# Nyström attention, expert FFN and GLU in one kernel: ScalarE first for steps that two engines can do, one-hot rows by one comparison a batch, batch 1's queries and keys in freed slots, new ranks for the planner

## The chip, the cores and the metric

The kernel runs on one core of a Trainium2 chip. The metric is the device time of one execution in microseconds (us), given as the median of three runs. The core has a matrix engine (TensorE, PE in the profile; PEld is its weight load), VectorE (DVE), ScalarE (ACT), GpSimd (POOL) and a queue engine, SyncE (SP), which here only issues DMAs and loads registers. PE, DVE and ACT read and write PSUM, the small memory in which matmuls accumulate; a 2 KB piece of it is a bank.

## The reference, cut to what matters

Four batches of 576 tokens with 8 heads of 64; 32 landmarks; an inverse by six iterations; then every token goes to the expert with the largest router logit (8 experts, at most 576 tokens each), through that expert's FFN, and what comes out through a gated layer (GLU).

```python
    A = sm(q, k_lm)
    Bm = sm(q_lm, k_lm)
    C = sm(q_lm, k)
    Z = ...
    for _ in range(6):
        Z = 2 * Z - Z @ Bm @ Z
    return (A @ Z @ C @ v).astype(np.float32)
...
    expert_idx = np.argmax(logits, axis=1)
...
    h = np.maximum(np.einsum('ecd,edf->ecf', disp, w1), 0.0)
    y = np.einsum('ecf,efd->ecd', h, w2)
...
            out[i] = gate_w[i] * y[expert_idx[i], pos[i]]
...
    gate = 1.0 / (1.0 + np.exp(-(x @ w_gate)))
    val = x @ w_val
    return (gate * val @ w_out).astype(np.float32)
```

## The kernel before, in words

**Stages.** First the attention, batch by batch, then blocks of up to 576 tokens of one expert through FFN and GLU. With these inputs three blocks have work: the *lead* block, whose tokens come from batch 0 alone and whose FFN starts while the later batches are still in attention; block 1; and one pass of a loop over the rest. The matmuls of blocks work on values split into a high and a low part, three products for one.

**Names of the attention.** For every batch `load_qk` brings q and k from memory in tiles named `qk` (or `slot`), `load_v` brings v (`early<-in_v`). PE transposes them (`pt<-ident,qk`), and the result is copied to `qT` and `kT`. Landmark sums are made on GpSimd (`s`). Scores are the matmuls `pa`, `pb` and `pc`, with row maxima through `pm`/`pnb`, exponentials `ea`, `eb` and `ec`, transposes `pct` copied to `ct`, and products with v in `pv`, copied to `cp`. The inverse's iterations alternate `py` (copied to `y`), `pu` and an update of `z`. `px` are the rows of the attention's output, scaled by the gate into `xt` and stored to memory (`x_rows`, and `x_lead` for batch 0).

**Routing.** For each batch the place of every token in the expert lists is worked out on VectorE, and a table of token numbers is made by a matmul of two one-hot matrices, `ptb<-hi,lo`. For each of six token columns there is one `hi` (which of 160 table columns) and one `lo` (which of 128 partitions). Once batch 0's table stands, SyncE reads the lead expert's number into a register, its weights are loaded (`w_raw`), and GpSimd gathers the lead block's rows by five indirect DMAs (`slot<-x_lead`).

**Blocks.** FFN: `mm<-xa,ws` and the like go through three PSUM banks. GLU: for every hidden tile a gate product and a value product go to a bank each; ScalarE takes the sigmoid of the gate product (`sg<-mm`), VectorE multiplies it with the value product (`sg<-mm,sg`), both split it, and `acc<-ws,...` is its product with the output weights. `ws_68` to `ws_71` and others hold split weights, made from `early` or `w_raw`. While the first GLU runs, its weights arrive as `raw_g`, `raw_v` and `raw_o` in an interleaved layout, and ScalarE separates and rounds them (`ACTIVATE raw_g<-raw_g`); `narrow` is the code for that. At the end of a block, `o_tile<-acc` copies the sums and `out<-o_tile` scatters them.

**What sets the order.** No order is written by hand. Every piece of work is a Python generator, and the class `Streams` runs them all against a clock of its own. Each `yield` names the engine and the things that the next step needs. `start` works out when the step could begin, `go` takes the one with the least planned start plus `SLACK` (0.003) times its rank from the table `URGENCY`, and `settle` adds the planned costs. Ranks so differ by some hundredths of a microsecond. A step for engine `any` may run on VectorE or ScalarE; before, it goes to the one that could begin it first. `fill_up` puts matmuls that compute nothing (`idle<-ones,ident`) into planned gaps of PE when the planned activity of the array is low. The order on each engine is thus fixed when the program is built, and an instruction waits for whatever stands ahead of it in its engine's row. All those instructions have line 88 in the profile. DMAs keep their own lines: 820 q and k, 833 v, 855 zeros, 490 interleaved weights, 557 expert weights, 1486 attention rows, 422 gathers, 723 scatters.

**Zeros.** The output has rows that no block writes. `zero_rows` stores zeros over the whole output in six DMAs of 768 KB, from a tile in the attention's own pool; before, it is spawned when batch 1's v is loaded and waits for the first load of the last batch's q.

**Buffers for q and k.** Batch 0 loads into eight `slot` tiles that are later used by the blocks; the other batches load into `qk` tiles from a pool of few, and each load needs one of these free (`raw`).

Of the kernel before, what the change touches and what calls it, by code (L numbers as in the profile page):

```python
# [10 lines left out]
F32 = mybir.dt.float32  # L11
F32R = mybir.dt.float32r
# [15 lines left out]
    sums=20,  # L28
    landmarks=30,
    transposes=0,  # L30
    inverse=4,
    scores=8,
    context=3,
    back=3,
    weights=15,
    rows=6,
    lead_rows=1,
    lead_loads=4,
    lead_split=15,
    lead=20,  # L40
    narrow=25,
# [51 lines left out]
class Streams:  # L93
# [5 lines left out]

    LAG = 0.2  # L100
    SAME = 0.13
# [99 lines left out]
    def settle(self, at, engine):  # L201
        first = True
        for what, name, value, columns in self.log:
            if what == "run":
# [7 lines left out]
                if name == "pe":  # L212
# [6 lines left out]
                    self.recent.append((at, columns))  # L219
                at += value  # L220
# [51 lines left out]
def tile_attention_moe_glu(  # L272
# [55 lines left out]
    wt = [wsp.tile([128, 2, 4, 128], F32R, name=f"ws{i}") for i in range(4)]  # L328
    actx = ExitStack()
# [156 lines left out]
    def narrow(dst, src, name):  # L486
# [4 lines left out]
        on.took("sp", 1.9)  # L491
# [50 lines left out]
    def expert_loads(b, number, at, split_urgency, first=0, until=KF + 2 * KD, needs=()):  # L542
# [4 lines left out]
        for i in range(first, until):  # L547
# [11 lines left out]
            run.took("sp", 0.95)  # L559
# [202 lines left out]
    with actx:  # L762
# [4 lines left out]
        zeros = ap.tile([128, 128], F32, name="zeros")  # L767
        nc.gpsimd.memset(zeros, 0.0)
# [41 lines left out]
        def load_qk(b):  # L810
            for w, src in enumerate((q, k)):
                for i in range(H // 2):
                    yield "sp", *(["raw"] if b else [])
                    if b == 0:
# [9 lines left out]
                    run.took("sp", 0.85)  # L824
# [5 lines left out]
        def load_v(b):  # L830
# [3 lines left out]
            run.took("sp", 3.4)  # L834
# [7 lines left out]
            if b == 1:  # L842
                run.spawn(zero_rows(), 200)
# [4 lines left out]

        def zero_rows():

            rows = out.rearrange("(p r) d -> p (r d)", p=128)
            for c in range(6):
                n = N // 128 * D // 6
                yield "sp", f"raw{B - 1}00"
                nc.sync.dma_start(
                    rows[:, c * n : (c + 1) * n].rearrange("p (x d) -> p x d", d=128),
                    zeros.unsqueeze(1).broadcast_to([128, n // 128, 128]),
                )
                run.took("sp", 2.2)

        def transposes(b):

            halves = []
            for w in range(2):

                s1 = None
                for g in range(2):
                    for jj in range(3):
# [14 lines left out]
                        if jj == 2 and b:  # L883
                            run.release("raw", "raw")
                        run.later(
# [346 lines left out]
        def back(b):  # L1232
# [140 lines left out]
            dve.tensor_copy(cf, ci[:, 1:3])  # L1373
            for j in range(J):
# [195 lines left out]
    def free_slots(**kinds):  # L1570
        run.slots.update({kind: [0.0] * n for kind, n in kinds.items()})
# [108 lines left out]
```

## Time and profile before

| what | us |
|---|---|
| median of three runs | 683.87 |
| lowest and highest run | 681.34, 688.35 |
| the profiled execution | 686.8 |
| its span, first to last instruction | 682.8 |
| PE busy in the span | 647.4 (95%) |
| DVE, ACT, POOL busy | 400.8, 286.3, 99.3 |

The profiled execution is one more execution, of 686.8 us, of which 4.0 us lie outside the span. A busy time adds up the stretches in which an engine had an instruction in hand. The granted clock is the TensorE clock as a share of full speed, 2.4 GHz; at half of it, 1.2 GHz, a matmul takes longer.

### The profile page before, as it was taken

What the parts mean: (1) busy time and instruction counts of PE and PEld (TensorE: products, weight loads), DVE (VectorE), ACT (ScalarE), POOL (GpSimd) and SP (SyncE); (2) the same over time, 40 slices, a digit from 0 to 9 for tenths busy, and PEclk for the clock granted to TensorE, in tenths of its full rate; (3) what the DMA queues carried; (4) which work ended last, traced back from release to release, by engine and by line L of the source; (5) the groups of instructions that cost most, each with busy time, mean ns of one, the idle gap of its engine ahead of it and who ended that gap; (6) DMA issues with size and microseconds to landing.
All of it is one profiled execution on the core that took longest, in us unless ns stands there. A gap on an engine that the chain in (4) does not pass through costs nothing.

```text
span 682.8 us, 14185 instructions
## 1 busy us (share of the span) xinstructions
PE 647.4 (95%) x5628; PEld 573.9 (84%) x5628; DVE 400.8 (59%) x1045; ACT 286.3 (42%) x644; POOL 99.3 (15%) x165
## 2 busy tenths in 40 slices
PE   7898879999997999999999899999999999999995
PEld 4466447688897999999999799999989999999994
DVE  7678859988777878786534443334435244434432
ACT  3424245544346666664433433333334234323331
POOL 3473466110011000000002400000020030000002
PEclk9999989999999999999999999999999999999999
DMA  8572999714376575544001300000034120000001
GB/s 212 119 176 78 263 234 272 229 33 134 116 227 190 169 219 177 155 143 136 1 1 38 103 1 0 1 1 1 1 116 141 30 70 1 0 1 1 1 1 70
DMA packets 64897, 65.94 MB, mean 97 GB/s; under 512 B 3513, under 2 KB 59841, under 8 KB 64833
## 3 DMA queue, kind: packets, MB, share of 16 engines
q1 hardware_dynamic: 62160, 56.78, 29.4%
q0 software_dynamic: 2672, 8.27, 3.9%
q8 instruction: 45, 0.74, 0.5%
q14 instruction: 20, 0.16, 0.1%
HBM read 50.87 MB, written 14.16 MB: 95 GB/s over the span
## 4 chain that ended last, share of the span: by engine, by line
PE 65%; issue 18%; DVE 7%; DMA 5%; ACT 2%; POOL 1%; SPq 1%; POOLq 0%; DVEq 0%; ACTq 0%
PE mm L88 44%; PE acc L88 11%; DMA qk<-in_q 3%; PE pt L88 2%; DMA out<-o_tile,idx_now 1%; PE pc L88 1%; SPq L820 1%; PE pa L88 1%; DVE xt L88 1%; PE pv L88 1%; DMA qk<-in_k 1%; PE pct L88 1%; PE px L88 1%; DVE ea L88 1%; PE idle L88 1%
## 5 line engine op out<-in xcount | busy, mean ns | idle before, releaser
L88 PEld LDWEIGHTS mm<-xb,ws 128*128 128x128 f32 x1344 | 189.9, 189 | 13.1 <-ACT ws L88 2.9
L88 PE MATMUL mm<-xb,ws 128*128 128x288 f32 x1344 | 197.3, 297 | 3.2 <-ACT ws L88 2.2
L88 PE MATMUL mm<-xa,ws 128*128 128x288 f32 x960 | 142.6, 300 | 5.1 <-ACT sg L88 4.7
L88 PEld LDWEIGHTS mm<-xa,ws 128*128 128x128 f32 x960 | 133.7, 190 | 11.1 <-ACT sg L88 5.0
L88 PE MATMUL acc<-ws,slot 128*128 128x512 f32 x476 | 130.5, 393 | 0.0
L88 PEld LDWEIGHTS acc<-ws,slot 128*128 128x128 f32 x476 | 82.3, 188 | 9.2
L88 DVE TENSOR_TENSOR sg<-mm,sg 128x288 f32<-128x288 f32 x72 | 32.8, 455 | 91.3 <-PE mm L88 90.7
L88 PE MATMUL mm<-slot,ws 128*128 128x288 f32 x576 | 79.5, 296 | 0.0
L88 PEld LDWEIGHTS mm<-slot,ws 128*128 128x128 f32 x576 | 76.9, 188 | 1.1 <-issue 0.5
L88 ACT CAST slot<-sg 128x288 fp32r<-128x288 f32 x68 | 29.4, 432 | 80.1 <-DVE sg L88 80.1
L88 DVE TENSOR_TENSOR ws<-wo_res,ws 128x512 fp32r<-128x512 f32 x30 | 20.8, 692 | 48.6 <-ACT ws L88 48.6
L88 ACT CAST ws<-wo_res 128x512 fp32r<-128x512 f32 x30 | 18.6, 621 | 70.7 <-PE acc L88 69.3
L88 DVE TENSOR_TENSOR slot<-sg,slot 128x288 fp32r<-128x288 f32 (+2 forms) x102 | 33.5, 354 | 17.2 <-ACT slot L88 17.2
L723 POOL DMA_INDIRECT out<-o_tile,idx_now x10 | 10.2, 1018 | 223.1 <-DVE o_tile L88 215.5
L422 POOL DMA_INDIRECT slot<-x_rows,idx_next x10 | 10.5, 1054 | 214.3 <-ACT sg L88 163.4
L88 DVE TENSOR_TENSOR ws<-w_raw,ws 128x512 fp32r<-128x512 f32 x50 | 34.7, 695 | 11.2 <-ACT ws L88 10.9
L88 ACT ACTIVATE sg<-mm 128x288 f32<-128x288 f32 x72 | 29.4, 409 | 28.1 <-PE mm L88 28.0
L88 ACT CAST ws<-w_raw 128x512 fp32r<-128x512 f32 x50 | 30.8, 618 | 17.7 <-PE mm L88 17.2
L88 ACT ACTIVATE slot<-mm 128x288 fp32r<-128x288 f32 x48 | 19.6, 409 | 21.6 <-PE mm L88 21.5
L88 DVE SCALAR_TENSOR_TENSOR slot<-mm,slot 128x288 fp32r<-128x288 f32 x48 | 21.6, 450 | 6.1 <-ACT slot L88 5.8
L88 DVE TENSOR_TENSOR xb<-mm,xb 128x288 fp32r<-128x288 f32 (+2 forms) x21 | 10.5, 500 | 23.0 <-ACT xb L88 22.8
L88 PE MATMUL pt<-ident,qk 96*128 96x96 f32 x144 | 19.9, 265 | 3.8 <-DMA qk<-in_q 2.9
(262 smaller groups left out, 829.4 us busy)
## 6 DMA issues: line engine op xcount, KB each, us to landing
w_raw<-in_moe_w SPq DMA_DIRECT2D x50, 256.0 KB, 3.2
raw_g<-in_moe_w_gate SPq DMA_DIRECT2D x12, 512.0 KB, 3.9
raw_v<-in_moe_w_val SPq DMA_DIRECT2D x12, 512.0 KB, 5.6
raw_o<-in_moe_w_out SPq DMA_DIRECT2D x12, 512.0 KB, 3.8
early<-in_v SPq DMA_DIRECT2D x4, 1152.0 KB, 12.1
x_rows<-xt SPq DMA_DIRECT2D x12, 384.0 KB, 6.1
out<-zeros SPq DMA_DIRECT2D x6, 768.0 KB, 7.0
qk<-in_q SPq DMA_DIRECT2D x12, 288.0 KB, 4.4
```

Source lines behind the costliest of these rows:

```text
L88: return getattr(self.engine, op)(*args, **kwargs)
L422: nc.gpsimd.indirect_dma_start(rows[c][0:n], None, src[:, :], bass.IndirectOffsetOnAxis(ap=idx[0:n, c : c + 1], axis=0), bounds_check=n_sr ...
L723: scatter = nc.gpsimd.indirect_dma_start(out[:, :], bass.IndirectOffsetOnAxis(ap=idx[0:n, c : c + 1], axis=0), o[0:n], None, bounds_check= ...
L820: nc.sync.dma_start(t.rearrange("p h j d -> p h (j d)"), src[b, 2 * i : 2 * i + 2].rearrange("h (p j) d -> p h (j d)", j=J),)
```

## The change

Six edits, in the order of the diff.

1. `URGENCY` has new ranks (all but `load`, `transposes` and `context`).
2. The planner: an `any` step goes to ScalarE unless VectorE could begin it over 0.6 us earlier (`SPARED`); time planned on GpSimd puts off planned work of VectorE by 0.3 of it (`SHARED`); PE behind PE has no planned gap; and some planned costs of SP are higher.
3. The tile of zeros lies in the base pool.
4. Batch 1's q and k go to the eight slots, each as soon as batch 0's transposes of that tile are done (`turned0..`), instead of to the pool.
5. `zero_rows` is spawned ahead of the second part of the order, and its DMAs wait until the last of the interleaved output weights is done (`narrow_o11`).
6. `hi` is made for all six columns by one comparison on a 96 x 6 x 160 tile instead of by six of 96 x 160.

```diff
 URGENCY = dict(
     load=4,
-    sums=20,
-    landmarks=30,
+    sums=40,
+    landmarks=5,
...
-    narrow=25,
+    narrow=3,
...
+    SPARED = 0.6
     LAG = 0.2
+    SHARED = 0.3
...
         def begin(engine):
-            return max(ready + (self.SAME if engine == last else self.LAG if last else 0), self.free[engine])
+            return max(ready + (0 if engine == last == "pe" else self.SAME if engine == last else self.LAG if last else 0), self.free[engine])
 
         if engine == "any":
-            engine = min("dve", "act", key=begin)
+            engine = "dve" if begin("dve") + self.SPARED < begin("act") else "act"
...
+                if name == "pool":
+
+                    self.free["dve"] = max(self.free["dve"], at) + self.SHARED * value
...
+    zeros = base.tile([128, 128], F32, name="zeros")
+    nc.gpsimd.memset(zeros, 0.0)
...
-                    yield "sp", *(["raw"] if b else [])
-                    if b == 0:
+
+                    yield "sp", *(["raw"] if b > 1 else []), *([f"turned0{w}{i // 2}"] if b == 1 else [])
+                    if b < 2:
...
-            if b == 1:
-                run.spawn(zero_rows(), 200)
...
+            yield ("dve",)
+            hi = wk.tile([P, J, NCOL], F32R, tag="hi", name=f"hi{b}", bufs=1)
+            dve.tensor_tensor(
+                hi,
+                iota_c[0:P].unsqueeze(1).broadcast_to([P, J, NCOL]),
+                cf[:, 1].unsqueeze(2).broadcast_to([P, J, NCOL]),
+                ALU.is_equal,
+            )
...
-                hi = wk.tile([P, NCOL], F32R, tag="hi", name=f"hi{b}{j}", bufs=2)
...
-                dve.tensor_scalar(hi, iota_c[0:P], cf[:, 1, j : j + 1], None, ALU.is_equal)
...
+    def zero_rows():
...
+            yield "sp", f"narrow_o{KG - 1}"
...
+    run.spawn(zero_rows(), 200)
     run.spawn(first_units(), 0)
```

What stands on the engines changes with it. In the whole program ScalarE has 703 instructions instead of 638 and VectorE 987 instead of 1072; the fills (`idle`) are 29 with 11,031 columns instead of 21 with 5,942.

ScalarE at the first sigmoid of the lead block, before. `raw_g` are interleaved gate weights, `ws` split expert weights, the table load is what the sigmoid needs:

```order
L88 CAST xa<-mm 128x288 x2
L88 ACTIVATE raw_g_3593<-raw_g_3593 128x512
L88 CAST ws_3497<-early 128x512
L88 ACTIVATE raw_g_3593<-raw_g_3593 128x512
L88 ACTIVATE raw_g_3601<-raw_g_3601 128x512
L88 CAST ws_70<-early 128x512
L88 ACTIVATE raw_g_3601<-raw_g_3601 128x512
L88 ACTIVATE raw_g_3603<-raw_g_3603 128x512
L88 CAST ws_71<-early 128x512
L88 ACTIVATE raw_g_3603<-raw_g_3603 128x512
L88 CAST ws_3498<-early 128x512
L88 ACT_TABLE_LOAD
```

The same place now, up to the second sigmoid:

```order
L88 CAST xa<-mm 128x288
L88 CAST ws_3486<-early 128x512
L88 ACT_TABLE_LOAD
L88 ACTIVATE sg<-mm 128x288
L88 ACTIVATE raw_g_3563<-raw_g_3563 128x512
L88 CAST ws_70<-early 128x512
L88 CAST early_gv_3484<-sg 128x288
L88 ACTIVATE raw_g_3563<-raw_g_3563 128x512
L88 CAST ws_71<-early 128x512
L88 ACTIVATE raw_g_3565<-raw_g_3565 128x512 x2
L88 CAST ws_3487<-early 128x512
L88 ACTIVATE sg<-mm 128x288
```

The separation of the gate weights moved from ahead of the first sigmoid to between it and the second.

PE in batch 0's score products and batch 1's transposes, before (`pc` is batch 0's, `pt` batch 1's):

```order
L88 MATMUL pc_372<-kT_251,bd_167 64x288 x2
L88 MATMUL pc_377<-kT_278,bd_167 64x288 x2
L88 MATMUL pt_384<-ident,qk_276 128x96 x2
L88 MATMUL pt_384<-ident,qk_332 128x96 x2
L88 MATMUL pc_391<-kT_251,bd_167 64x288 x2
L88 MATMUL pt_399<-ident,qk_276 128x96 x2
```

The same place now:

```order
L88 MATMUL pc_377<-kT_250,bd_167 64x288 x2
L88 MATMUL pc_380<-kT_280,bd_167 64x288 x2
L88 MATMUL pc_388<-kT_250,bd_167 64x288 x2
L88 MATMUL pc_392<-kT_280,bd_167 64x288 x2
L88 MATMUL pt_406<-ident,slot_341 128x96 x2
L88 MATMUL pt_406<-ident,slot_367 128x96 x2
```

Batch 0's products stand ahead of batch 1's transposes, which read slots.

SP at the lead expert's weights, before:

```order
L855 DMA out<-zeros 128x12x128
L545 TENSOR_LOAD lead
L545 ISA x2
L557 ISA
L557 DMA w_raw<-in_moe_w 128x4x128
L820 DMA qk_1581<-in_q 96x2x384
```

SP behind the last interleaved weights, now:

```order
L498 DMA raw_o_5039<-in_moe_w_out 128x1024
L1577 DMA out<-zeros 128x12x128 x6
L553 TENSOR_LOAD lists
L553 ISA x2
L565 ISA
L565 DMA w_raw<-in_moe_w 128x4x128
```

The six stores of zeros left the attention for one place behind the last `raw_o`, ahead of the next expert's weights.

## Rows read from the trace of the kernel before

**Rows 1.** The page: busy time by engine, share of the span, instructions.
```profile
PE 647.4 (95%) x5628; PEld 573.9 (84%) x5628; DVE 400.8 (59%) x1045; ACT 286.3 (42%) x644; POOL 99.3 (15%) x165
```
**Rows 2.** Busy time by stretch: PE, PEld, DVE, ACT, POOL, granted clock, DMA share, GB/s.
```profile
60.00:80.00 20.00, 16.61 (x282) 10.90 (x279) 18.30 (x69) 7.47 (x20) 10.97 (x22) 1.00 0.77 205
80.00:100.00 20.00, 15.21 (x195) 8.10 (x194) 9.50 (x38) 5.96 (x19) 8.88 (x14) 0.83 0.95 249
...
0.00:115.00 115.00, 98.38 (x1401) 64.06 (x1401) 85.18 (x291) 46.73 (x126) 58.64 (x127) 0.96 0.75 190
115.00:206.00 91.00, 89.09 (x1167) 75.37 (x1167) 76.78 (x267) 40.28 (x101) 11.45 (x13) 1.00 0.53 156
206.00:220.00 14.00, 9.25 (x58) 9.02 (x57) 10.37 (x21) 9.89 (x18) 0.96 (x1) 0.88 0.56 176
220.00:380.00 160.00, 159.96 (x1095) 152.45 (x1094) 106.72 (x217) 84.27 (x174) 7.37 (x8) 1.00 0.39 119
380.00:392.00 12.00, 9.51 (x52) 7.99 (x51) 6.78 (x12) 6.43 (x13) 5.20 (x3) 0.86 0.22 75
```
**Rows 3.** Waits of PE: line, releaser, us in total, times, longest.
```profile
PE mm L88 <- ACT sg L88: 4.7, 1, 4.7
PE pa L88 <- issue: 2.5, 1, 2.5
```
**Rows 4.** PE around the first sigmoid: start, us, operation, [idle before].
```profile
206.34 4.92 PE L88 MATMUL mm<-xa,ws 128*128 128x288 f32 x36
216.00 6.55 PE L88 MATMUL mm<-xa,ws 128*128 128x288 f32 x36 [4.75 <-ACT sg L88]
```
**Rows 5.** ScalarE in the same stretch.
```profile
207.94 0.40 ACT L88 CAST xa<-mm 128x288 fp32r<-128x288 f32 x1 [4.10 <-PE mm L88]
208.23 0.68 ACT L88 ACTIVATE raw_g<-raw_g 128x512 f32<-128x512 f32 x1
208.80 0.62 ACT L88 CAST ws<-early 128x512 fp32r<-128x512 f32 x1
...
214.24 1.28 ACT L88 ACT_TABLE_LOAD   x1
215.54 0.41 ACT L88 ACTIVATE sg<-mm 128x288 f32<-128x288 f32 x1
```
**Rows 6.** The chain that ended last, 56 to 82 us, by line.
```profile
by line: DVE ea L88 9.0%; DVE ra L88 7.9%; DVE hi L88 7.7%; issue 6.8%; DVE xt L88 6.4%; DVE lo L88 4.7%; DVE z L88 4.3%; PE idle L88 3.3%; ACT xt L88 3.2%; DVE scan L88 3.2%; DVE zt L88 2.6%; DVE ma L88 2.5%; PE pl L88 2.5%; PE pa L88 2.4%
```
**Rows 7.** Tiles xt and hi by engine: durations in ns, least, median, most.
```profile
L88 ACT ACTIVATE xt<-px,gates x30: 458/470/481, 63.5 to 190.1; 96x256 f32<-96x256 f32 x30
L88 DVE TENSOR_SCALAR xt<-px,gates x18: 464/474/480, 63.0 to 189.5; 96x256 f32<-96x256 f32 x18
...
L88 DVE TENSOR_SCALAR hi<-iota_c,cf x24: 198/293/1190, 67.6 to 196.0; 96x160 fp32r<-96x160 f32 x24
```
**Rows 8.** VectorE, one product of two tensors over 576 elements.
```profile
71.56 0.71 DVE L88 TENSOR_TENSOR ea<-ea,ma 128x576 f32<-128x576 f32 x1
```
**Rows 9.** PE: a fill, and the first product of the lead block.
```profile
76.26 0.77 PE L88 MATMUL idle<-ones,ident 128*128 128x297 f32 x2
...
114.94 1.06 PE L88 MATMUL mm<-xa,ws 128*128 128x288 f32 x6
```
**Rows 10.** PE: a late load, and the change from the lead block to block 1.
```profile
24.57 0.39 PE L88 MATMUL pt<-ident,qk 96*128 96x96 f32 x2 [1.63 <-DMA qk<-in_q]
...
383.39 0.46 PE L88 MATMUL mm<-ident,slot 64*128 64x64 f32 x4 [0.99 <-DVE xa L88]
386.21 0.54 PE L88 MATMUL mm<-xb,ws 128*128 128x288 f32 x2 [1.24 <-ACT ws L88]
```
**Rows 11.** DMA from 70 to 130 us; SP and GpSimd at the end of the lead block.
```profile
DMA packets 18342, 15.73 MB, mean 262 GB/s; under 512 B 591, under 2 KB 17373, under 8 KB 18333
...
312.37 0.34 SPq L490 DMA_DIRECT2D raw_o<-in_moe_w_out  x1
...
377.03 1.04 POOL L723 DMA_INDIRECT out<-o_tile,idx_lead  x1 [0.30 <-issue]
```

More of the change, by code (lines that the diff above doesn't have):

```diff
@@ L27 @@
     load=4,
-    sums=20,
-    landmarks=30,
+    sums=40,
+    landmarks=5,
     transposes=0,
-    inverse=4,
-    scores=8,
+    inverse=1,
+    scores=10,
     context=3,
[L34 to L40, printed above, removed]
-    narrow=25,
+    back=2,
+    weights=37,
+    rows=12,
+    lead_rows=14,
+    lead_loads=18,
+    lead_split=40,
+    lead=21,
+    narrow=3,
 )
@@ L490, in narrow @@
         nc.sync.dma_start(raw, src)
-        on.took("sp", 1.9)
+        on.took("sp", 2.1)
         on.done(f"raw_{name}", 4.0)
@@ L558, in expert_loads @@
             w_raw[b, i] = raw
-            run.took("sp", 0.95)
+            run.took("sp", 1.1)
             run.done(f"w_raw_{b}{i}", 3.5)
@@ L765, in tile_attention_moe_glu @@
         ps = actx.enter_context(tc.tile_pool(name="ps", bufs=7, space=PSUM))
-        zeros = ap.tile([128, 128], F32, name="zeros")
-        nc.gpsimd.memset(zeros, 0.0)
         for dst in (x_dram[N : N + 1], x_lead[S : S + 1]):
@@ L823, in load_qk @@
                     )
-                    run.took("sp", 0.85)
+                    run.took("sp", 1.25)
                     st[b][f"raw{w}{i}"] = t
@@ L833, in load_v @@
             nc.sync.dma_start(vs.rearrange("p h j d -> p h (j d)"), v[b].rearrange("h (p j) d -> p h (j d)", j=J))
-            run.took("sp", 3.4)
+            run.took("sp", 5.0)
             if b == 0:
@@ L847, in load_v @@
                 run.spawn(load_v(b + 1), urgency("load", b + 1))
[L849 to L859, printed above, removed]
         def transposes(b):
@@ L882, in transposes @@
                             )
-                        if jj == 2 and b:
+                        if jj == 2 and b > 1:
                             run.release("raw", "raw")
+                        if jj == 2:
+                            run.done(f"turned{b}{w}{g}")
                         run.later(
@@ L1380, in back @@
                 )
-                yield ("dve",)
-                dve.tensor_scalar(hi, iota_c[0:P], cf[:, 1, j : j + 1], None, ALU.is_equal)
                 yield "pe", *(["bank"] if j == 0 else [])
@@ L1385, in back @@
                     ptb = pst([128, NCOL], f"ptb{b}")
-                pe.matmul(ptb, lo, hi, start=(j == 0), stop=(j == J - 1))
+                pe.matmul(ptb, lo, hi[:, j], start=(j == 0), stop=(j == J - 1))
             yield ("dve",)
@@ L1489, in row_store @@
                 )
-                run.took("sp", 1.1)
+                run.took("sp", 1.5)
             run.release("xt")
@@ L1568, in tile_attention_moe_glu @@
     accs = [accp.tile([128, D], F32, name=f"acc{c}") for c in range(TC)]
+    def zero_rows():
+        rows = out.rearrange("(p r) d -> p (r d)", p=128)
+        for c in range(6):
+            n = N // 128 * D // 6
+            yield "sp", f"narrow_o{KG - 1}"
+            nc.sync.dma_start(
+                rows[:, c * n : (c + 1) * n].rearrange("p (x d) -> p x d", d=128),
+                zeros.unsqueeze(1).broadcast_to([128, n // 128, 128]),
+            )
+            run.took("sp", 2.2)
     def free_slots(**kinds):
```

## The prediction

> **What bounds the kernel now.** I read the page's busy times first. TensorE has work in hand for 95% of the span, and no other engine for 60% [rows 1]. So time can come from three places only: the 35 us in which PE waits (span less 647.4), the stretches at half clock, and matmuls that compute nothing. The busy time by stretch says where they lie [rows 2]. Up to 115 us, where the lead block's first product starts [rows 9], PE is busy 98.4 of 115 us. From 115 to 206 it is busy 89.1 of 91, from 206 to 220 only 9.25 of 14 and at a mean clock of 0.88, from 220 to 380 all of 160 us. From 380 to 392 it lacks 2.5 us. The blocks' products, more than two thirds of the span, wait for nothing that the change moves; so whatever it brings must come from before 220 us, and a little from 380 to 392.
>
> The list of waits names the largest [rows 3]: one of 4.7 us for a sigmoid. The reader should then look at PE and ScalarE side by side there. PE runs 36 products into three banks from 206.34, is out of banks at 206.34 + 4.92 = 211.26, and goes on at 216.00; the next 36 take 6.55 us instead of 4.92, because the clock had fallen to half while it waited [rows 4]. ScalarE had been free of the FFN at 207.94 + 0.40, but its row has six separations of gate weights and four casts ahead of the table load, which starts only at 214.24 [rows 5].
>
> In the attention a different engine sets the pace. From 60 to 80 us VectorE is busy 18.3 of 20 us, ScalarE 7.5, PE 16.6 [rows 2], and the chain that ended last in 56 to 82 us is mostly VectorE: `hi` 7.7% and `xt` on VectorE 6.4% of these 26 us, 2.0 and 1.7 us [rows 6]. From 80 to 100 PE lacks 4.8 us and has a clock of 0.83, beside a DMA share of 0.95 [rows 2].
>
> **The change part by part.**
>
> *First sigmoid (ranks of the narrow weights).* The order now puts one cast between the last `xa` cast and the table load. By the rows of before: `xa` at 207.94, the next instruction can start 0.29 later at 208.23, one `ws` cast takes 0.62, the table load 1.28, the sigmoid 0.41 [rows 5], which ends at about 210.5. That is before 211.26, when PE needs the bank, so the wait of 4.75 us goes, and with it the 6.55 − 4.92 = 1.6 us of half clock [rows 4]. What is late next is the second sigmoid. Behind the first one stand four separations, three `ws` casts and one split. At the pace of the rows (a separation every 0.57 us, 208.23 to 208.80; the casts a little less, estimated 0.5 and 0.35) that is about 4.2 us, so that the second sigmoid ends near 210.5 + 4.2 + 0.4 = 215.1. PE has 24 more products in the two banks that the first sigmoid and VectorE's product free, 24/36 of 4.92 = 3.3 us, to 214.5. I take a new wait of 1.0 us, for a semaphore's way and a slow cast. Term: −4.75 − 1.6 + 1.0 = **−5.4 us**. Bounds: −6.4 with no new wait; −2 if it is long enough to bring the half clock back.
>
> *From the lead block to block 1.* PE waits 0.99 and 1.24 us there [rows 10] and lacks 2.5 us from 380 to 392, at a clock of 0.86 [rows 2]. All of the lead block's last products now stand together and the transposes behind them, two of them much later. The casts that free the weights still wait for the last product. I take −0.7, with bounds −2.5 (all of it goes) and +1 (the tiles to be copied come in one heap).
>
> *Batch 1's loads.* The wait for a q load at 24.57 held batch 0's `pc` back, because it stood behind a transpose of batch 1 [rows 10]. Now all four `pc` pairs come first, and the loads need no tile from the pool, but slots that batch 0's transposes have left. In exchange, a batch 1 load can't start before those transposes. Term −1, bounds −1.6 (the wait itself) and +1.
>
> *Steps to ScalarE, and `hi`.* Some 65 steps leave VectorE: 18 `xt` of 0.47 us, which take 0.47 on ScalarE too [rows 7], and as many shorter ones. Twenty-four `hi` comparisons (median 0.29 us [rows 7]) become four over 960 elements. No such instruction is in the trace. The nearest is a product of two tensors over 576 elements, 0.71 us [rows 8]; scaled by 960/576 it gives 1.2 us, against 6 × 0.29 = 1.8 before. But the first product in PE now waits for all of it, where before it waited for one column. Bounds: 0.7 (no dearer than 576 elements) and 1.8 (no gain). On the chain of 56 to 82 us, `hi` would lose some 0.8 of 2.0 us, and `xt` the 1.7 us that VectorE spends on it, as ScalarE has 12.5 us free of 20 [rows 2]. So some 2.5 us for this routing, and a second one, batch 1's, falls before or around 115 us: up to −5 us, and −7.3 if the whole of `hi` and `xt` left the chain in both (2 × 3.7).
>
> The Trainium skill speaks against this part: its page "ScalarE: Activation LUTs", section "Rules for kernel authors", says that multiplications and the like belong on VectorE, which per element is up to about three times as fast in bf16. By it the 18 `xt` would take up to three times 0.47 us on ScalarE, 17 us more work on that engine, the 1.7 us of the chain would stay, and the sum would come to about −8. The trace doesn't agree for this kernel's fp32 from PSUM: both take 0.47 us [rows 7], so I give this no weight in the sum.
>
> *Fills.* The planner now puts 29 instead of 21 fills, 11,031 instead of 5,942 columns, all ahead of the lead block's first product. A fill of 297 columns took 0.77 us in the trace [rows 9], 2.6 ns a column with its fixed part; 5,089 more columns are up to 13 us. They cost nothing where PE would have waited, and 16.6 us of the stretch to 115 were such waits [rows 2]; they cost all of it where the wait is gone in reality. Fills also keep the clock up: from 80 to 100 us it was 0.83, which is 3.4 us lost against full speed at most. I take it that three quarters of the 13 us, 9.8 us, stand in gaps that were idle before, and that the remaining 3.2 us are paid. Half of the clock's loss, 1.7, comes back.
>
> *Zeros.* Six stores of 768 KB are 4.7 of the 15.73 MB that were moved between 70 and 130 us [rows 11]. Without them the other loads there land sooner. Only the wait of 2.5 us put down to issue [rows 3] lies in that stretch and has no cause that the trace shows; I give 1.0 of it. Now they stand behind the last `raw_o` (312.37), nearly 65 us before the first scatter at 377.03 [rows 11], where DMA is idle enough; cost 0. If that cover were gone, they would hold the scatters, which PE doesn't wait for.
>
> The last three parts together: −4 for VectorE's chain (2.5 for the first routing, 1.5 of the second's 2.5, since that one lies partly behind 115 us, where PE is full), + 3.2 − 1.7 − 1.0, which gives −3.5. I take **−2.5**, since ScalarE's row also gets longer and stays in order. Bounds: −10 (7.3 + 1.7 + 1.0, no fill paid) and +13 (all fills paid, no gain).
>
> **Sum.** −5.4 − 0.7 − 1.0 − 2.5 = −9.6 us. The profiled execution would go from 686.8 to 677.2 us, its span from 682.8 to 673. It stands 2.9 us above the median of 683.87; on the median the same sum gives 674.3, and I say **675**.
>
> **The rivals.**
>
> *The fills eat the gain.* PE is bound in the attention too, so the chain's gain is filled with idle products and only the sigmoid's wait goes: 683.9 − 5.4 ± 1, about 679, which is within 1%. For it: PE is busy 98.4 of 115 us, and some of that is fills already. Against it: VectorE's 18.3 of 20 us from 60 to 80 shows that PE isn't what the chain waits for.
>
> *Slower: ScalarE's row becomes the bound of the attention.* ScalarE takes its row in order, and `any` steps now queue there up to 0.6 us longer before VectorE gets one. Where exponentials (`ec`, `ea`) stand behind `xt` and copies, each batch's scores come late; the planner answers with fills, and fills are paid. With all 13 us paid and 5.4 + 0.7 back it gives 683.9 + 13 − 6.1 = 691 us. It decides when more than 6 us of fills are paid and nothing of VectorE's chain comes back. For it: the number of fills nearly doubles, which says that the plan has longer gaps. Against it: ScalarE is busy 46.7 of the first 115 us [rows 2], and 65 more steps, none much longer than `xt`'s 0.47 us, add at most 31; a third stays free.
>
> *The second sigmoid takes the first one's place.* If the separations between them run slower than in the rows and PE's clock falls again, that place brings only 2 us, and with −4.2 elsewhere the time is 683.9 − 6.2, about 678. For it: the four separations and three casts are simply moved behind the first sigmoid. Against it: PE has 3.3 us of products to cover them.
>
> **How the numbers follow.** A measurement of this kernel tells about 1% from no change. My forecast, 667 to 676.5, has 0.53; the sigmoid rival 0.12 and the fills 0.23, both around 679, in part faster by over 1% (below 677); the slower one 0.12, of which 0.08 are over 690.7. Faster by over 1%: 0.53 + 0.07 = 0.60. Slower by over 1%: 0.08. The rest, 0.32, is within 1%. The range, 665 to 686, leaves out about 0.1 above and less than 0.1 below, where the whole of the chain's gain and no paid fill would bring the sum to about −18.
>
> **What would show it.** In the profile after, PE should have no wait over 2 us for `sg` near 210 us and 36 products at one pace around it; the mean clock from 206 to 220 should be near 1.0. VectorE should be busy less than 16.5 of the 20 us in which it now has 18.3, `hi` should take about 1.2 us, and the lead block's first product should start 2 to 5 us earlier than 114.94. Zeros should be issued behind 300 us with nobody waiting for them. I am wrong if that first product starts at 115 us or later with more `idle` time on PE, or if a new wait of 4 us for ScalarE stands between the first two sigmoids.

## The result, and the profile after

The changed kernel took 663.73 us (median of four runs, 662.93 to 664.78); the kernel before took 686.11 us beside it (four runs, 681.34 to 692.98). The ratio is 0.9693, with a 95% interval of 0.9648 to 0.9738: faster by 3.1%, 22 us. Ratios leave out the executions that fell into a slower state, medians don't. I had said 675 us, 665 to 686. The sign and the likeliest case were right, the gain that I forecast was less than half of what came, and the median lies 1.3 us below the low end of the range. The profiled execution took 663.88 us, its span 662.0.

The first stretch to look at is the one up to the first GLU product, because behind it little is different. It starts at 193.49 us instead of 206.34. These are the busy times up to that product, of the kernel before and then of the kernel after (columns as in [rows 2]: length, PE, PEld, DVE, ACT, POOL, granted clock, DMA share, GB/s):

```profile
0.00:206.34 206.34, 187.80 (x2569) 139.77 (x2570) 162.30 (x558) 87.01 (x226) 70.35 (x140) 0.98 0.65 176
```
```profile
0.00:193.49 193.49, 185.24 (x2584) 139.69 (x2585) 139.44 (x472) 103.94 (x291) 69.16 (x137) 1.00 0.60 160
```

PE's idle time fell from 206.34 − 187.80 = 18.5 us to 193.49 − 185.24 = 8.3 us. VectorE lost 23 us of work, ScalarE won 17. The clock is at full speed throughout. Now the fills (`idle`) in the same two stretches, before and after (columns: length, PE, PEld, clock, DMA share, GB/s):

```profile
0.00:206.34 206.34, 17.16 (x42) 7.60 (x42) 0.98 0.65 176
```
```profile
0.00:193.49 193.49, 26.64 (x58) 10.04 (x58) 1.00 0.60 160
```

Fills cost 9.5 us more. So the rest of PE's work, the same products in both orders (2569 − 42 = 2527 records before and 2584 − 58 = 2526 after), took 187.80 − 17.16 = 170.6 us before and 185.24 − 26.64 = 158.6 after. The 12.85 us are −10.3 of idle time, +9.5 of fills, and −12.0 of the same products in less time. The reader sees where that comes from in batch 0's score products, which the trace of the kernel after shows as one run (start, us, operation):

```profile
22.29 2.11 PE L88 MATMUL pc<-kT,bd 128*64 128x288 f32 x16
```

Before, the same `pc` stood in fours between transposes, and two of these fours ran while the clock was at half:

```profile
24.89 1.21 PE L88 MATMUL pc<-kT,bd 128*64 128x288 f32 x4
26.02 0.90 PE L88 MATMUL pt<-ident,qk 96*128 96x96 f32 x4
26.86 1.23 PE L88 MATMUL pc<-kT,bd 128*64 128x288 f32 x4
```

Two fours at half clock take 2.4 us; sixteen in one run at full clock take 2.1. Over the whole stretch the mean of a `pc` fell from 490 to 414 ns and that of a `pt` in slots or `qk` from about 268 to 252 ns.

How much of the 12.0 us is the clock's can be bounded. Ahead of the GLU it was below 1.00 before only from 80 to 100 us (0.83 [rows 2]) and from 20 to 40:

```profile
20.00:40.00 20.00, 17.68 (x293) 11.16 (x296) 14.27 (x46) 9.67 (x28) 11.12 (x23) 0.91 0.42 102
```

That is 2 × (0.17 + 0.09) × 20 = 10 us at half clock, in which products lose at most some 5 us against full clock. This is an estimate; the other 7 go with products of one kind standing together.

The stretches that the prediction spoke of, after (to hold against [rows 2]):

```profile
60.00:80.00 20.00, 19.50 (x375) 13.17 (x374) 16.62 (x65) 10.27 (x31) 8.86 (x17) 1.00 0.74 199
80.00:100.00 20.00, 18.84 (x338) 12.69 (x337) 15.10 (x63) 12.27 (x39) 10.56 (x15) 1.00 0.69 189
...
206.00:220.00 14.00, 14.00 (x99) 12.96 (x98) 12.89 (x26) 8.92 (x18) 0.00 (x0) 1.00 0.67 203
```

From 60 to 100 us PE went from 31.8 to 38.3 of 40 us, and its clock from a mean of 0.83 in the second half to 1.00. The wait for the first sigmoid [rows 3, 4] is gone. PE at that place, after:

```profile
193.49 0.42 PE L88 MATMUL mm<-xa,ws 128*128 128x288 f32 x2
194.15 10.33 PE L88 MATMUL mm<-xa,ws 128*128 128x288 f32 x76 [0.23 <-DVE ws L88]
```

The lead block's first product, at 114.94 us before [rows 9], starts earlier too. After:

```profile
106.07 1.06 PE L88 MATMUL mm<-xa,ws 128*128 128x288 f32 x6
```

The waits of PE that are left over the whole span, after (line, releaser, us, times, longest):

```profile
PE idle L88 <- POOL ident masks.py:199: 2.0, 1, 2.0
PE mm L88 <- DVE xa L88: 1.9, 2, 1.3
PE mm L88 <- DVE ws L88: 1.5, 4, 0.9
PE mm L88 <- ACT ws L88: 1.5, 2, 1.0
```

None is over 2.0 us. The first is a wait at the start of the program, for a constant. From block lead to block 1, PE waits once, 1.3 us for `xa`, where it waited 0.99 and 1.24 us [rows 10].

The one comparison that replaces six, after (times in ns, least, median, most), with the six of [rows 7] for comparison:

```profile
L88 DVE TENSOR_TENSOR hi<-iota_c,cf x4: 1145/1149/1157, 73.1 to 180.3; 96x960 fp32r<-96x960 f32 x4
```

And the zeros, behind the last `raw_o`, some 40 us before the first scatter at 360.03:

```profile
308.15 0.34 SPq L498 DMA_DIRECT2D raw_o<-in_moe_w_out  x1
308.54 13.26 SPq L1577 DMA_DIRECT2D out<-zeros  x6
323.26 6.61 SPq L565 DMA_DIRECT2D w_raw<-in_moe_w  x4
```

### The profile page after: what moved, and what is told of

The parts are those of the page before. It is cut to its first block, busy times and chain, and to the rows that moved or that the text cites. A ratio compares the mean times of both kernels' runs of the same rounds, so it can differ in the third digit from the quotient of the medians.

```text
span 662.0 us, 14225 instructions
## 1 busy us (share of the span) xinstructions
PE 641.1 (97%) x5644; PEld 571.3 (86%) x5644; DVE 382.2 (58%) x960; ACT 308.2 (47%) x709; POOL 98.1 (15%) x165
## 4 chain that ended last, share of the span: by engine, by line
PE 72%; issue 17%; ACT 3%; DMA 3%; DVE 2%; POOL 1%; POOLq 0%; DVEq 0%; SPq 0%; ACTq 0%
PE mm L88 46%; PE acc L88 11%; PE idle L88 3%; PE px L88 2%; PE pt L88 2%; PE pa L88 1%; DMA slot<-in_q 1%; PE pc L88 1%; DMA out<-o_tile,idx_now 1%; PE pu L88 1%; PE py L88 1%; PE pv L88 1%; POOL out L731 1%; PE pl L88 1%; POOL slot L430 1%
## 5 line engine op out<-in xcount | busy, mean ns | idle before, releaser
L88 PE MATMUL mm<-xb,ws 128*128 128x288 f32 x1344 | 184.1, 295 | 3.7 <-DVE xa L88 1.9
L88 PEld LDWEIGHTS mm<-xb,ws 128*128 128x128 f32 x1344 | 180.9, 188 | 7.5 <-DVE xa L88 2.3
L88 PE MATMUL mm<-xa,ws 128*128 128x288 f32 x960 | 136.6, 297 | 1.4 <-DVE ws L88 1.1
L88 PEld LDWEIGHTS mm<-xa,ws 128*128 128x128 f32 x960 | 129.4, 188 | 4.7 <-DVE ws L88 1.6
L88 PE MATMUL acc<-ws,slot 128*128 128x512 f32 x476 | 114.4, 391 | 0.0
L88 PEld LDWEIGHTS acc<-ws,slot 128*128 128x128 f32 x476 | 87.5, 188 | 16.6
L731 POOL DMA_INDIRECT out<-o_tile,idx_now x10 | 10.2, 1016 | 225.2 <-DVE o_tile L88 217.1
L88 PE MATMUL idle<-ones,ident 128*128 128x512 f32 (+13 forms) x58 | 26.6, 556 | 2.0 <-POOL ident masks.py:199 2.0
L88 ACT CAST ws<-wv_res 128x512 fp32r<-128x512 f32 x30 | 18.6, 620 | 12.9 <-PE mm L88 12.7
```

The costliest lines, as they stand in the source:

```text
L88: return getattr(self.engine, op)(*args, **kwargs)
L731: scatter = nc.gpsimd.indirect_dma_start(out[:, :], bass.IndirectOffsetOnAxis(ap=idx[0:n, c : c + 1], axis=0), o[0:n], None, bounds_check= ...
```

## The experiments

Which edit brought the 12.85 us? Theory O says that it is the order of PE's products, V that VectorE was relieved, Z that the zeros left a stretch in which DMA was full; and the fills are either what keeps the clock or a pure cost. The first four kernels keep the changed order row for row on every engine and take one part back in what is issued.

The twelve runs come in three sets of four, each set on a chip of its own. The median of the kernel before was 688.25 us beside the first four runs (13 executions), 683.70 beside the second four (19) and 685.89 beside the third (17). A difference to the changed kernel is therefore given twice where it matters: by the medians, and by the ratios to before. No time of the changed kernel beside these sets is on record, nor the chip on which it took 663.73 us, so whatever differs between chips is in these differences. This turns out to matter, as the second set shows.

**Zeros back among the attention's loads.** The six stores are issued on SP behind loads of batch 3 and behind rows 2 and 3, without a planned cost:

```diff
-            yield "sp", f"narrow_o{KG - 1}"
+            yield "sp", ("raw310", "raw311", "raw312", "raw313", "rows2", "rows3")[c]
...
-            run.took("sp", 2.2)
```

> The changed kernel with its order kept row for row, but the six stores of zeros put back among the attention's loads on SP. Theory Z (the gain came from taking 4.7 MB out of the stretch in which DMA was full): waits and half clock near 85 to 100 us come back, so 668 to 672 us instead of 663.7. Theory O (the gain came from the order in which PE's products stand): 663 to 665 us.

675.04 us, 0.9814 of before (0.9748 to 0.9881). Some 11 us of the gain go by the medians, 8 by the ratios; the time is 3 us above theory Z's range. But the profile doesn't show late loads. It shows a stand-still of PE and then half clock (start, us, operation, idle before):

```profile
92.09 0.37 PE L88 MATMUL pvt<-sel,cp 128*64 128x64 f32 x4
95.44 0.48 PE L88 MATMUL pvt<-sel,cp 128*64 128x64 f32 x4 [2.98 <-issue]
95.86 2.18 PE L88 MATMUL pt<-ident,qk 96*128 96x96 f32 x12
```

Twelve such `pt` take 1.16 us in the kernel after and 2.18 here: half clock. PE waits for `cp` on ScalarE, and ScalarE for something that the trace calls remote:

```profile
ACT cp L88 <- remote: 4.7, 1, 4.7
```

This "remote" is PE itself. `cp` waits for a semaphore that PE's products alone raise. In the trace's record of semaphores it rises at 91.35 us and next at 95.10, though the `pg` and `pa` that raise it had ended at 91.5 and 92.1; `cp` starts at 95.12. The view names no releaser because the product lies so far back. Such late counts of PE stand beside GpSimd's indirect DMAs, here the lead block's five gathers. Up to them the run loses nothing: its first gather is issued earlier than that of the changed kernel (this run, then the kernel after):

```profile
89.27 1.15 POOL L430 DMA_INDIRECT slot<-x_lead,idx_now  x1 [7.89 <-DVE wg L88]
```
```profile
90.03 1.15 POOL L430 DMA_INDIRECT slot<-x_lead,idx_now  x1 [7.88 <-DVE wg L88]
```

**Every third step back to VectorE.** The plan still counts the step on ScalarE; the instruction goes to VectorE:

```diff
     def copy(self, dst, src):
-        if self.engine == "act":
+        if self.third(("copy", (dst, src))):
+            self.dve.engine.tensor_copy(dst, src)
+        elif self.engine == "act":
             self.act.copy(dst, src)
```

> The changed kernel with its order kept row for row, but every third of the steps that two engines can do is issued to VectorE instead of ScalarE (61 of 184; before it was 65 on VectorE). Theory V (the gain came from taking work off VectorE): the first GLU product, now at 193.5 us, moves at least 5 us towards the old 206.3, so 669 to 676 us. Theory O: 663 to 666 us.

680.4 us, 0.9893 (0.9815 to 0.9971). Most of the gain goes, more than theory V had (669 to 676). Here too a step waits 4.4 us for "remote" near 95 us, now on VectorE (`lg`), and the clock is at half in parts of 84 to 88 and of 98 to 105 us. What VectorE's work alone does is seen ahead of that: the first gather is issued at 92.49 us, 2.5 us later than in the changed kernel. So theory V has the sign; its size can't be told from the stand-still's.

**Six comparisons for `hi`.**

```diff
-            dve.tensor_tensor(
-                hi,
...
+            run.log.append(("run", "dve", *COSTS["dve"]("tensor_tensor", (hi,))))
+            for j in range(J):
+                nc.vector.tensor_scalar(hi[:, j], iota_c[0:P], cf[:, 1, j : j + 1], None, ALU.is_equal)
```

> The changed kernel with its order kept, but each batch's one-hot rows are made by six comparisons of 96x160 one after the other, in the place of the one of 96x960. Theory V: 6 x 0.29 = 1.7 us instead of 1.15 on VectorE's chain for each batch that is not hidden, 1 to 2 us in all, so 665 to 666 us. Theory O: 663 to 665 us, not to be told from no change.

673.89 us (670.91 to 677.57), 0.9788 (0.9712 to 0.9864). With an edit worth 1 to 2 us on VectorE, 10 us go by the medians and 6.5 by the ratios. Neither theory had that. Three windows from 84 to 108 us show why; first this kernel, then the kernel after:

```profile
84.00:90.00 6.00, 6.00 (x175) 3.98 (x173) 3.29 (x17) 3.74 (x13) 0.90 (x1) 1.00 0.42 123
90.00:96.00 6.00, 4.04 (x40) 2.58 (x37) 0.29 (x2) 0.40 (x1) 4.28 (x5) 0.83 0.91 248
96.00:108.00 12.00, 11.91 (x82) 8.38 (x80) 6.30 (x32) 4.64 (x13) 3.99 (x8) 0.52 0.32 86
```
```profile
84.00:90.00 6.00, 5.91 (x162) 3.81 (x161) 3.08 (x17) 4.32 (x15) 0.00 (x0) 1.00 0.42 128
90.00:96.00 6.00, 6.00 (x102) 4.33 (x102) 4.46 (x25) 3.60 (x10) 4.75 (x5) 1.00 0.89 244
96.00:108.00 12.00, 11.48 (x138) 9.07 (x138) 9.84 (x34) 9.96 (x27) 9.22 (x21) 1.00 0.84 218
```

From 90 to 96 us VectorE and ScalarE stand almost still (0.29 and 0.40 us of work in 6) while GpSimd works through the lead block's five gathers, and PE's clock is near half for the 12 us that follow. In these, PE does 82 products instead of 138. ScalarE waits to copy `pgt`, whose products had ended at 89.82:

```profile
89.07 0.75 PE L88 MATMUL pgt<-at,wg 128*32 128x288 f32 x8
```
```profile
93.47 0.40 ACT L88 COPY lg<-pgt 128x288 f32<-128x288 f32 x1 [4.31 <-remote]
```

PE's count for them is recorded at 93.45. Here too the first gather is issued earlier than in the changed kernel, at 89.11.

**No fills.** The plan counts them, nothing is issued:

```diff
-        run.fill = lambda n: pe.matmul(
-            idle[:, 0:n], ident, ones[:, 0:1].broadcast_to([128, n]), start=True, stop=True
-        )
+        run.fill = lambda n: run.log.append(
+            ("run", "pe", *COSTS["pe"]("matmul", (idle[:, 0:n], ident, ones[:, 0:1].broadcast_to([128, n]))))
+        )
```

> The changed kernel with its order kept, but without the 29 matmuls that compute nothing (26.6 us of PE time). If they stand in PE's real gaps and keep the clock: half clock shows in several places before 120 us and the time is 666 to 675 us. If they only take PE's time where it would have worked: 655 to 660 us. If neither: 662 to 665 us.

683.42 us (677.75 to 691.64, ten runs), 0.9935 (0.9886 to 0.9984). Taking 26.6 us of PE work away made the kernel 17 (ratios) to 20 us (medians) slower. The clock from 40 to 120 us:

```profile
40.00:60.00 20.00, 16.03 (x237) 9.56 (x235) 9.81 (x37) 7.51 (x26) 12.55 (x26) 0.74 0.62 148
60.00:80.00 20.00, 19.07 (x287) 14.79 (x287) 9.18 (x42) 10.47 (x32) 5.54 (x12) 0.66 0.45 105
80.00:100.00 20.00, 17.03 (x319) 10.66 (x315) 14.30 (x51) 8.80 (x29) 6.66 (x9) 0.74 0.61 187
100.00:120.00 20.00, 17.08 (x162) 12.11 (x163) 8.68 (x43) 8.83 (x23) 11.14 (x21) 0.83 0.50 136
```

Fills stand in real gaps and keep the clock; the rival by which they eat the gain falls. The half clock of the first two lines lies ahead of this run's gathers (from 98.94 us). The time is above the range that I gave this case (666 to 675); the stand-still is in this run too (ScalarE's `lg`, 5.5 us for "remote").

All four have a stand-still during the gathers with half clock at it or behind it, and in two of them it can't come from a delay, since they reach the gathers 0.8 to 0.9 us earlier than the changed kernel. Theory G names the gathers as its source.

**The kernel before with plain loads.** The lead block's rows come from tokens 0 to 575 by SP's own DMAs; the choice of rows by the index list is left out:

```diff
-            gather(tiles, idx_now, x_lead, S)
+            for c, (t0, n) in enumerate(TILES):
+                nc.sync.dma_start(tiles[c][0:n], x_lead[t0 : t0 + n])
```

> The kernel before, but the lead block's rows come by five plain loads on SP in the place of GpSimd's five indirect gathers (it takes the tokens 0 to 575 instead of the lead expert's, so it leaves the choice of rows out). Theory G (in the runs so far some engine stands still for 3 to 5 us with no releaser shown while those gathers run, PE with it, and the clock falls to half behind that): the waits put down to issue at 89 to 93 us and the half clock behind them go, so about 5 us faster, 0.99 of before. Theory O: the gathers are not it, 1.00.

685.17 us, 1.0038 (0.9993 to 1.0083): no gain. The waits put down to issue are gone from the list, but the clock fell at other places, some 24 us at half up to 120 us instead of 10:

```profile
80.00:100.00 20.00, 18.68 (x260) 12.63 (x259) 14.50 (x52) 10.42 (x29) 7.69 (x16) 0.84 1.05 293
100.00:120.00 20.00, 19.54 (x198) 14.42 (x198) 15.13 (x53) 9.94 (x25) 9.17 (x17) 0.73 0.75 211
```

**Six comparisons and plain loads.** The same edit on the changed kernel with six comparisons:

> The changed kernel with hi made by six comparisons, as in the run before, and the lead block's rows by plain loads on SP (the choice of rows is left out). Theory G: the 4.3 us of stand-still at 89 to 93.5 us and the half clock up to 107 us go, so 663 to 666 us. If the six comparisons themselves cost the time: 672 to 676 us.

666.20 us (665.18 to 667.72), 0.9729 (0.9646 to 0.9811): 7.7 us faster than with the gathers by the medians. By the ratios it is 4, and these intervals overlap. In the windows PE has its full clock and is busy 6.00 of 6 us where it stood still:

```profile
90.00:96.00 6.00, 6.00 (x84) 4.28 (x74) 4.71 (x24) 3.20 (x9) 2.95 (x6) 1.00 1.07 285
96.00:108.00 12.00, 8.94 (x107) 7.25 (x104) 6.44 (x27) 8.75 (x24) 5.32 (x12) 1.00 0.63 149
```

This is what theory G said for the changed order, with about 2.5 us left for the six comparisons. But the two runs belong to two sets, and the next two runs take the conclusion away. This run also has PE idle for 3 us from 96 to 108, with the clock at 1.00 throughout.

**The ranks, both ways.** The changed kernel with the old table, and the kernel before with the new one:

```diff
-    sums=40,
-    landmarks=5,
...
-    narrow=3,
+    sums=20,
+    landmarks=30,
...
+    narrow=25,
```

> The changed kernel with the old table of ranks, everything else new. Theory O (the order made by the ranks carries most of the gain): the wait before the first sigmoid is there again and the time is 676 to 684 us. If the other five edits carry it: 664 to 670 us.

> The kernel before with the new table of ranks alone. Theory O: 0.975 to 0.985 of before, as the wait before the first sigmoid goes and PE's products stand in longer runs. If the ranks only fit together with the other edits: 0.99 to 1.01.

710.82 us, 1.0400 (1.0295 to 1.0505); and 692.07 us, 1.0087 (1.0043 to 1.0130). The first is beyond both cases that I gave; the second lies where I put it if the ranks only fit together with the other edits (0.99 to 1.01). Old ranks with the new rules are 27 us slower than the kernel before; new ranks with the old rules are 6 us slower by the ratio, 8 by the medians. In the second, PE waits 9.9 us once for a load of k, and the clock from 100 to 120 us is 0.65:

```profile
PE pt L88 <- DMA qk<-in_k: 9.9, 1, 9.9
```

The ranks are no gain of their own. They fit one set of rules and of loads.

These two kernels have the five gathers again:

```profile
95.09 1.15 POOL L430 DMA_INDIRECT slot<-x_lead,idx_now  x1 [0.55 <-DMA qk<-in_k]
```
```profile
95.03 1.15 POOL L422 DMA_INDIRECT slot<-x_lead,idx_now  x1 [1.19 <-DVE m L88]
```

Yet no wait in them is put down to "remote", and no count of PE is recorded more than 0.3 us late in the whole span. The same is true of the two runs with plain loads, which kept the other blocks' 30 indirect DMAs. So the second set is free of the stand-still with the gathers and without them. In every trace of the first and the third set PE's counts come late beside the lead block's gathers, by 1.6 to 4.1 us at most, and late again beside later indirect DMAs. What parts the traces is the set, and with it the chip; theory G isn't shown. The trace of the kernel before has such a count (2.2 us), that of the changed kernel none over 0.3 us.

**The rank of the narrow weights alone.** The kernel before with `narrow=3`:

```diff
-    narrow=25,
+    narrow=3,
```

> The kernel before with the one rank narrow = 3 instead of 25. Its order on ScalarE has the table load right behind the last xa cast. If the first sigmoid's wait is worth what it measures (4.75 us and 1.6 us at half clock): no wait for sg over 1 us and 0.990 to 0.992 of before. If a new wait takes its place: 0.995 to 1.00.

686.55 us, 0.9991 (0.9959 to 1.0024): nothing. The order did what it should: the first sigmoid starts right after the table load. But a new wait came, on VectorE:

```profile
205.38 1.59 PE L88 MATMUL mm<-xa,ws 128*128 128x288 f32 x10 [0.20 <-ACT sg L88]
212.23 8.35 PE L88 MATMUL mm<-xa,ws 128*128 128x288 f32 x44 [5.25 <-DVE xa L88]
```

The last low part of `xa` stands on VectorE behind work on gate weights, and that behind a load that lands at 207.4:

```profile
207.41 0.65 ACT L88 ACTIVATE raw_g<-raw_g 128x512 f32<-128x512 f32 x1 [1.57 <-DMA raw_g<-in_moe_w_gate]
```
```profile
211.39 0.42 DVE L88 TENSOR_SCALAR cvt_g<-raw_g 128x512 uint32<-128x512 uint32 x1
211.72 0.45 DVE L88 TENSOR_TENSOR xa<-mm,xa 128x288 fp32r<-128x288 f32 x1
```

In the changed kernel that same step runs at 195.25, ahead of all work on gate weights.

**The planner's rules undone.** The changed kernel with `SPARED`, `SHARED` and the missing gap taken back:

```diff
-            return max(ready + (0 if engine == last == "pe" else self.SAME if engine == last else self.LAG if last else 0), self.free[engine])
+            return max(ready + (self.SAME if engine == last else self.LAG if last else 0), self.free[engine])
...
-            engine = "dve" if begin("dve") + self.SPARED < begin("act") else "act"
+            engine = min("dve", "act", key=begin)
...
-    SHARED = 0.3
+    SHARED = 0
```

> The changed kernel with the planner's three rules undone (steps for two engines to the one that can begin first, no GpSimd time on VectorE, the old gap between PE's products), ranks and all else new. If the clock decides: the granted clock from 0 to 220 us tells the time, some 1 us for each 1 us at half clock, and at full clock throughout 664 to 667 us. If ScalarE's share itself decides: 670 us or more at whatever clock.

691.75 us, 1.0101 (1.0059 to 1.0143). By the sum over the windows of 20 us to 220 us (the missing part of the clock, twice) it ran some 14 us at half clock, as did the kernel before, but it is 28 us behind the changed one. So the clock doesn't tell it all: PE waits for `lo` (3.4 us), `xa`, `s` and the first sigmoid (2.2 to 2.5 us each) as well. The three rules were undone together; which of them counts is open.

**Batch 1's loads in the pool's tiles.**

```diff
-                    yield "sp", *(["raw"] if b > 1 else []), *([f"turned0{w}{i // 2}"] if b == 1 else [])
-                    if b < 2:
+                    yield "sp", *(["raw"] if b else [])
+                    if b == 0:
...
-                        if jj == 2 and b > 1:
+                        if jj == 2 and b:
```

> The changed kernel with batch 1's q and k loaded into the pool's tiles as before, all else new. If the early slots matter: PE waits 2 to 4 us for loads of q near 25 us and the clock falls there, 667 to 675 us. If not: 663 to 666 us.

680.35 us, 0.9893 (0.9843 to 0.9943): 14 to 17 us of the gain go, more than expected, and not near 25 us. The order differs from there on, and from 100 to 120 us the clock is at half almost throughout. Late counts of PE beside the gathers are in this run too, so their share isn't separated:

```profile
100.00:120.00 20.00, 20.00 (x189) 15.25 (x193) 7.93 (x38) 9.89 (x25) 9.20 (x21) 0.53 0.47 116
```

**Every twelfth step back to VectorE.**

```diff
-        if self.turn % 3:
+        if self.turn % 12:
```

> The changed kernel with its order kept row for row, every twelfth of the steps that two engines can do issued to VectorE (15 of 184). If the cost goes with the number moved (a third cost 16 us): 668 us. If it comes in steps, with the stand-still and the half clock near 90 us or without: 663 to 665 us without, 671 us or more with.

673.66 us (672.02 to 677.76), 0.9840 (0.9796 to 0.9883). A quarter as many steps as in the run with a third, and 10 of its 17 us (10 of 14 by the ratios). By these numbers the cost doesn't go with the number of steps. The stand-still is there (VectorE's `lg`, 3.6 us for "remote", beside gathers from 89.19 to 95.6), and PE's 24 `pv` come in portions:

```profile
90.16 0.67 PE L88 MATMUL pv<-early,ct 96*32 96x64 f32 x8
91.25 0.32 PE L88 MATMUL pv<-early,ct 96*32 96x64 f32 x5 [0.42 <-issue]
91.98 0.33 PE L88 MATMUL pv<-early,ct 96*32 96x64 f32 x5 [0.41 <-issue]
92.70 0.32 PE L88 MATMUL pv<-early,ct 96*32 96x64 f32 x5 [0.39 <-issue]
```

The likelier reading is another. This run, the one with zeros back and the one with six comparisons are three unlike edits, and all lie within 1.4 us, at 673.66 to 675.04. Each issues its first gather earlier than the changed kernel (89.19 us here), and each is of a set whose traces all have the stand-still. So most of these 10 us is probably the stand-still's and not the edit's; a third of the steps would then cost some 6 us of its own (680.4 less 674, an estimate). The changed kernel on the same chip would settle it; that wasn't run.

None of the versions beat the changed kernel's 663.73 us.

## Why the prediction was right, and where its sizes were off

**First sigmoid, −5.4.** Right in place and near in size. The 72 products that took 16.2 us (from 206.34 to 216.00 + 6.55, [rows 4]) take about 10.2 now (the first 72 of the 78 shown above): −6.0. The stand-still has little part in it: the kernel before with plain loads is free of that, and PE waits 4.2 us for the sigmoid there. My new wait of 1.0 us for the second sigmoid didn't come: it starts at 200.99 and the products run through. But the reason I gave, one rank, was too small. With that rank alone the time stays the same, since a load and VectorE's `xa` are next. The term needs `xa` to stand ahead of the work on gate weights as well, as it does in the changed kernel.

**Block lead to block 1, −0.7.** One wait of 1.3 us where two of 2.2 us together and half clock were; all that lies behind the first GLU products, this place among it, is 20.8 − 12.85 − 6.0 = 2 us less. Right in sign, a little small.

**Batch 1's loads, −1, and the steps to ScalarE, `hi`, fills and zeros, −2.5 together: the step that failed.** These terms, −3.5, measured −12.85. Three of their parts were mis-sized.
The first is the clock: I gave half of 3.4 us back for 80 to 100 us. In the kernel before it was at half for some 10 us before the GLU (0.91 from 20 to 40 us, 0.83 from 80 to 100), and all of that went, worth up to 5 us.
The second is PE's work, which I took as fixed. The same products took 12 us less, at full clock (the 5 us just named) and in longer runs of one kind.
The third are the fills: I priced them at 13 us and charged 3.2. They took 9.5 more, while the idle time fell by 10.3, and without them the kernel is 17 to 20 us slower.
The wait of 2.5 us put down to issue, of which the zeros' term took 1.0, is such a stand-still: PE's `pm` ended at 90.45 us and its count is recorded at 92.62. The changed kernel's trace doesn't have it, but no run shows that the zeros or another edit took it away.

**What I added that can't be added.** Each term stood for itself. Taken back one at a time, the zeros cost 11 us by the medians (8 by the ratios), a third of the steps 17 (14), six comparisons 10 (6.5), the loads' tiles 17 (14), the planner's rules 28 (28) and the ranks 47 (48): together over five times the whole gain. So there are no shares to hand out. Nor is the list the edits' doing alone: all of it but the ranks comes from the two sets whose traces have the stand-still. Free of that are the ranks, and the fills with their half clock ahead of the gathers. What the changed kernel's trace shows is a state, a PE that hardly waits and has its full clock (0.998 over the span). Six comparisons with plain loads had it too (666.20 us, 0.999), in the set without the stand-still. Whether the changed kernel has it on the other chips isn't shown.

**The rivals.** That fills eat the gain was wrong. That ScalarE would be the bound was wrong: it is busy 103.9 of 193.5 us. The second sigmoid took no one's place here; in the kernel before with one rank changed, VectorE's `xa` did.

**The signs I named.** The first lead product starts at 106.07, 8.9 us earlier, well beyond what I had said (2 to 5): two thirds of the 12.85 us are won by then. One fill stands behind it, at 118.87; I had put all of them ahead. VectorE is busy 16.6 us from 60 to 80, not under 16.5. `hi` takes 1.15 us; I had said 1.2. The zeros stand at 308.5 us, and their landing keeps nobody waiting.

**The skill's rule.** The rule of the Trainium skill ("ScalarE: Activation LUTs", "Rules for kernel authors"), that multiplications and the like belong on VectorE, would have spoken for the run with a third of the steps there, as far as these are multiplications and not copies. That run is 2 to 2.5% slower than the changed kernel, though how much of this is the stand-still's isn't separated; it reaches the gathers 2.5 us later. At the step itself neither engine is faster (`xt` takes 0.47 us on both [rows 7]).

**What stays open.** Why PE's counts come late beside GpSimd's indirect DMAs in nine of the traces (before, and all of the first and third set) and not in the other five. The chip parts the twelve runs, but no kernel's trace is kept from two chips. Loads of instruction code don't explain it: from 100 to 106 us of the run without fills, while ScalarE waits, DMA moves 299 packets of the gathers' queue and 70 of that of SP's loads, and none of the queues that load instructions. It also stays open how much of the 22 us the edits would bring on a chip with the stand-still. The kernel before took 683.70 us in the set without it and 685.89 and 688.25 in the others, so by this estimate some 5 us of the 22 at most could be its absence; the versions nearest to the changed kernel there are at 0.979 to 0.984 of before. Nor did any run disturb the changed order where no edit touches it.

## What to carry to other kernels

Where one engine is busy nearly all of the span and its clock can fall, price a wait together with the half clock that follows it: here 4.75 us of wait for the sigmoid brought 1.6 us more. Run the changed kernel beside every version of it, on the same chip; three unlike edits seemed to cost 10 us each here, and their traces point to one thing that all three runs shared. Don't sum edits of a planned order one by one; ask whether the plan still has waits at all, and look at the granted clock window by window before and after. Work that computes nothing can be the cheapest part of a plan, if it stands in real gaps.

## What the runs showed of the hardware that was not expected

While GpSimd works through five indirect DMAs (1.0 us each), a count that PE raises at the end of a product can be recorded 1.6 to 4.1 us late, in nine of the fourteen traces. The engine that waits for it stands 3.3 to 5.5 us in six of these, with a releaser that the views call "remote", and in some PE's products come in portions of five every 0.73 us. In the other five traces no count of PE is over 0.3 us late, though three of them have the same five gathers and all of them later indirect DMAs.

The same matmuls in the same number took 158.6 instead of 170.6 us of PE time, from full clock and from standing beside their like: sixteen `pc` in one run 2.11 us, four alone 0.71 us at full clock and 1.21 to 1.23 at half. These times count the end of a product that overlaps the next; from start to start it is 2.05 us for the sixteen and 0.64 for the four.
